# Tile 0 in three pieces through norm, transpose and copy, and whole x tiles on two load queues

## The chip, the cores and the metric

The kernel runs on one core of one Trainium2 chip. The metric is the device time in microseconds (us); lower is better. Engines are named as in the profile: PE is TensorE (PEld its weight loads), DVE is VectorE, ACT is ScalarE, POOL is GpSimd, SP is SyncE, which here only issues transfers (DMAs).

## The reference

A layernorm without affine weights feeds two branches, a linear attention block and a dense block with gelu, and both are added to the input:

```python
def _A_ref(x, wqkv, wo):          # H = 32 heads of 20
    q, k, v = ...                 # x @ wqkv
    phi = lambda t: jnp.where(t > 0, t + 1, jnp.exp(t)) + 1e-6
    pq, pk = phi(q), phi(k)
    kv = jnp.einsum("bhsd,bhse->bhde", pk, v)
    z = jnp.einsum("bhsd->bhd", pk)
    num = jnp.einsum("bhqd,bhde->bhqe", pq, kv)
    den = jnp.einsum("bhqd,bhd->bhq", pq, z)[..., None] + 1e-6
    ...                           # (num / den) @ wo

def _B_ref(x, w1, b1, w2, b2):
    h = _gelu(jnp.einsum("bsd,df->bsf", x, w1) + b1)
    return jnp.einsum("bsf,fd->bsd", h, w2) + b2

xn = _layernorm(x, axis=-1)
return x + _A_ref(xn, A_wqkv, A_wo) + _B_ref(xn, B_w1, B_b1, B_w2, B_b2)
```

x is 2048 tokens by 640 features in bf16; W1 is 640 by 1536 and W2 1536 by 640.

## The kernel before

The 2048 tokens are 16 tiles of 128. A tile of x is loaded with tokens on the 128 partitions, normalised over its 640 features (`xn_tm`), and transposed so that features lie on the partitions (`xnT`, five blocks of 128 features). W1 is held as five rows of blocks, W1 row k being the 128 features that multiply block k of `xnT`, by 1536 outputs. The hidden layer has 12 groups of 128 outputs (`jb`).

All instructions are recorded through a planner, which keeps one list per engine in the order in which the code calls it, and derives the waits from the resources that a step reads and writes. It doesn't reorder: what stands ahead in an engine's list runs first there.

Only the first steps matter for the change. They are:

- Loads. Tile 0 comes in two parts (L272 to L274): columns 0 to 383 by the SP queue and columns 384 to 639 by the ACT queue. Behind its part SP issues tile 1, W1 rows 0, 1 and 2, tile 2, W1 row 3, tile 3, W1 row 4, tiles 4 to 7.
- PE starts with matmuls on constants (`filler`, L319, and L445, which also starts the accumulation in banks 0 to 5), until tile 0 is ready.
- Layernorm of a tile: `ln_half` twice on DVE (a BATCH_NORM_STATS2 on a part of the columns, L351, after the first of which POOL adjusts a number, L354), `ln_aggr` (DVE L359, then on POOL the power -0.5 that gives `rstd`, L361), and `ln_norm` (DVE L373). Tile 0 is normalised in two pieces, of 256 and 384 columns.
- `transp2` (L336) transposes a tile on PE, blocks 0 and 1 into PSUM bank 6 and blocks 2 to 4 into bank 7. `copy2` moves them to `xnT`, the first part on ACT (L344), the second on DVE (L345). Tiles 0 and 1 go this way. Tile 2 is transposed by `transp` (L381) and copied on DVE (L389); from tile 3 on a DMA transposes.
- The head of the hidden layer is written row by row: `hk` (L431) does, for one group jb, the matmuls of the rows `ks` on one or two tiles. Groups 2b and 2b+1 share bank b; when row 4 is done, ACT applies gelu (L438).

The order of PE's work is the list `plan` (L464 to L468): for tile 0 row 0 of W1 over 12 groups; "B1", a small transpose of b1 (L325) with its copy on ACT; row 1; "T1", tile 1's transposes; row 2; for tile 1 rows 0, 1, 2; for both tiles row 3 on groups 0 to 7; "T2", tile 2's transposes; the remaining rows. Then come packs of four groups for tiles 2 and 3 (`h_pack`, L415), and units of 256 or 512 tokens (`h_unit`, L400), up to about 59 us. The attention and the output follow. PSUM banks of these later groups are dealt out in a ring by `take`, which `at(n)` sets.

The order of DVE's work ahead of the plan is the sequence of calls at L450 to L459; more follows at "T1" and "T2" inside the loop over the plan (L490 to L507).

Of the kernel before, what the change touches and what calls it, by code (L numbers as in the profile page):

```python
# [6 lines left out]
ACT = mybir.ActivationFunctionType  # L7
P = 128
FP32 = mybir.dt.float32
BF16 = mybir.dt.bfloat16  # L10
# [102 lines left out]
def bass_parallel_sum__linear_attn_block__dense_activation_gelu__prompt_kernel(  # L113
    nc: bass.Bass, A_x, A_wqkv, A_wo, B_x, B_w1, B_b1, B_w2, B_b2, out):
    Batch, S, D = A_x.shape
    F = B_w1.shape[1]
    assert Batch == 1 and D == 640 and F % P == 0 and S % 512 == 0
    NT = S // P
# [3 lines left out]
    DT = D // P  # L122
# [3 lines left out]
    HW = D // 2  # L126
# [11 lines left out]
    Pl = Planner(nc)  # L138
    R_ = Pl.res

    with contextlib.ExitStack() as es:
# [3 lines left out]
        x_in = xPK  # L145
        PK = xPK
        xn_tm = sb("xn_tm", [P, NT, D], BF16)
        xnTf = sb("xnT", [P, DT * S], BF16)
        xnT = xnTf[:].rearrange("p (k s) -> p k s", k=DT)
# [22 lines left out]
        ident = sb("ident", [P, P], BF16)  # L172
# [5 lines left out]
        stats = sb("stats", [P, 4, 12], FP32)  # L178
# [19 lines left out]
        B_ = [R_("bank%d" % i) for i in range(8)]  # L198
# [10 lines left out]
        def bank(b, lo=0, hi=512):  # L209
            return ps[:, b * 512 + lo: b * 512 + hi]  # L210

        def halves(ap):
            return ap.rearrange("p (a n) -> p a n", a=2)

        r_x = [[R_("x%d_%d" % (t, i)) for i in range(2 if t == 0 else 1)] for t in range(NT)]
        r_xr = [R_("xr%d" % c) for c in range(NC)]
        r_xb = [R_("xb%d" % t) for t in range(NT)]
        r_xn = [[R_("xn%d_%d" % (t, i)) for i in range(2 if t == 0 else 1)] for t in range(NT)]
        r_xnT = [[R_("xnT%d_%d" % (t, i)) for i in range(2 if t < 2 else 1)] for t in range(NT)]
        r_W1 = [R_("W1_%d" % k) for k in range(DT)]  # L220
        r_Wk = R_("Wk")
        r_Wq, r_Wv, r_W2 = R_("Wq"), R_("Wv"), R_("W2")
# [3 lines left out]
        r_ident, r_small, r_ones, r_masks, r_hmask = (  # L226
            R_("ident"), R_("small"), R_("ones"), R_("masks"), R_("hmask"))
        r_stats = [[R_("stats%d_%d" % (i, h)) for h in range(2)] for i in range(4)]
# [20 lines left out]
        xv = A_x.rearrange("b s d -> (b s) d")  # L249
# [5 lines left out]
        v = "vector"  # L255
        s_ = "scalar"
        pe = "tensor"

        def dma(eng, dst, src, writes, reads=()):
            Pl.ins(eng, lambda e: e.dma_start(dst, src), reads=reads, writes=writes, dma=True)  # L260
# [4 lines left out]
        def dma_x(t, n):  # L265
            dma("sync", x_in[:, t:t + n, :], xv[t * P:(t + n) * P, :].rearrange("(t p) d -> p t d", p=P),
                sum(r_x[t:t + n], []))

        def dma_w1(k):
            dma("sync", W1[:, k, :], w1v[:, k, :], [r_W1[k]])  # L270

        XA = 3 * P  # L272
        for i, (lo, hi) in enumerate(((0, XA), (XA, D))):
            dma(("sync", s_)[i], x_in[:, 0, lo:hi], xv[0:P, lo:hi], [r_x[0][i]])  # L274
        dma_x(1, 1)
        dma_w1(0)
        dma_w1(1)
        dma_w1(2)
# [15 lines left out]
               reads=[r_ident], writes=[r_ident])  # L294
# [28 lines left out]
        def b1_step():  # L323
            b = take(1)
            Pl.ins(pe, lambda e: e.transpose(bank(b).bitcast(BF16)[:, 0:JT], b1tmp[:], ident[:JT, :JT]),  # L325
                   reads=[r_b1tmp, r_ident], writes=[B_[b]])
            Pl.ins(s_, lambda e: e.activation(b1c[:], bank(b).bitcast(BF16)[:, 0:JT], ACT.Copy),
                   reads=[B_[b]], writes=[r_b1c])

        KA = 2  # L330
        TC = KA * P

        def transp2(t, b0, b1):
            for lo, hi, b in ((0, KA, b0), (KA, DT, b1)):
                pT = bank(b).bitcast(BF16)
                Pl.ins(pe, [(lambda e, k=k, pT=pT, lo=lo: e.transpose(  # L336
                    pT[:, (k - lo) * P:(k - lo + 1) * P], xn_tm[:, t, k * P:(k + 1) * P], ident[:]))
                    for k in range(lo, hi)], reads=[r_xn[t][0 if lo == 0 else -1], r_ident], writes=[B_[b]])

        def copy2(t, b0, b1):  # L340
            tok = slice(t * P, (t + 1) * P)
            pA = bank(b0).bitcast(BF16)[:, 0:TC].rearrange("p (k q) -> p k q", q=P)
            pB = bank(b1).bitcast(BF16)[:, 0:D - TC].rearrange("p (k q) -> p k q", q=P)
            Pl.ins(s_, lambda e: e.activation(xnT[:, 0:KA, tok], pA, ACT.Copy), reads=[B_[b0]], writes=[r_xnT[t][0]])  # L344
            Pl.ins(v, lambda e: e.tensor_copy(xnT[:, KA:DT, tok], pB), reads=[B_[b1]], writes=[r_xnT[t][1]])  # L345

        def ln_half(t, h):
            s = t % 4
            cut = XA if t == 0 else HW
            lo, hi = ((0, cut), (cut, D))[h]  # L350
            Pl.ins(v, lambda e: e.bn_stats(stats[:, s, 6 * h:6 * h + 6], x_in[:, t, lo:hi]),  # L351
                   reads=[r_x[t][min(h, len(r_x[t]) - 1)]], writes=[r_stats[s][h]])
            if h == 0:
                Pl.ins(g, lambda e: e.tensor_single_scalar(stats[:, s, 2:3], stats[:, s, 2:3], D * EPS, ALU.add),  # L354
                       reads=[r_stats[s][0]], writes=[r_stats[s][0]])

        def ln_aggr(t):
            s = t % 4
            Pl.ins(v, lambda e: e.bn_aggr(aggr[:, s, :], stats[:, s, :]),  # L359
                   reads=r_stats[s], writes=[r_aggr[s]])  # L360
            Pl.ins(g, lambda e: e.tensor_tensor(out=rstd[:, t:t + 1], in0=aggr[:, s, 1:2], in1=mhalf[:], op=ALU.pow),  # L361
                   reads=[r_aggr[s], r_small], writes=[r_rstd[t]])

        def ln_stats(t):
            ln_half(t, 0)
            ln_half(t, 1)
            ln_aggr(t)

        def ln_norm(t):
            s = t % 4  # L370
            for i, r in enumerate(r_xn[t]):
                lo, hi = (0, D) if len(r_xn[t]) == 1 else ((0, TC), (TC, D))[i]
                Pl.ins(v, lambda e, lo=lo, hi=hi: e.tensor_scalar(  # L373
                    xn_tm[:, t, lo:hi], x_in[:, t, lo:hi], aggr[:, s, 0:1], rstd[:, t:t + 1],
                    ALU.subtract, ALU.mult),
                    reads=r_x[t] + [r_aggr[s], r_rstd[t]], writes=[r])
# [19 lines left out]
        def h_unit(t0, n, jb):  # L396
# [12 lines left out]
               writes=[r_b1c])  # L409
# [14 lines left out]
        def at(b):  # L424
            ring[0] = b

        def hk(t, n, jb, ks):
            b = jb // 2
            o = (jb % 2) * 2 * P + t * P
            tok = slice(t * P, (t + n) * P)  # L430
            Pl.ins(pe, [(lambda e, k=k: e.matmul(  # L431
                bank(b, o, o + n * P), W1[:, k, jb * P:(jb + 1) * P], xnT[:, k, tok],
                start=False, stop=(jb % 2 == 1 and k == DT - 1))) for k in ks],
                reads=[r_W1[k] for k in ks] + [r_xnT[u][0 if max(ks) < KA else 1] for u in range(t, t + n)],
                writes=[B_[b]])
            if DT - 1 in ks and jb % 2:
                for i in range(2):
                    Pl.ins(s_, lambda e, i=i, jb=jb - 1 + i: e.activation(  # L438
                        HG[:, jb, tok], bank(b, i * n * P, (i + 1) * n * P), ACT.Gelu_apprx_tanh, bias=b1c[:, jb:jb + 1]),
                        reads=[B_[b], r_b1c], writes=[r_HG[u][jb - 1 + i] for u in range(t, t + n)])  # L440
# [3 lines left out]
        for b in range(6):  # L444
            Pl.ins(pe, lambda e, b=b: e.matmul(  # L445
                bank(b), nc.const_aps.tensor(1.0, [P, P], BF16), pm[:].broadcast_to((P, 512)), start=True, stop=False),
                reads=[r_pm], writes=[B_[b]])
# [3 lines left out]
        ln_half(0, 1)  # L451
        ln_aggr(0)
        ln_half(1, 0)
        ln_norm(0)
        ln_half(1, 1)
        ln_aggr(1)
        transp2(0, 6, 7)
        copy2(0, 6, 7)
        ln_norm(1)  # L459

        h_list = lambda t, n, lo, hi: [(t, n, jb) for jb in range(lo, hi)]
        k_list = lambda t, n, ks, lo=0, hi=JT: [(t, n, jb, ks) for jb in range(lo, hi)]
# [26 lines left out]

        for u in plan:  # L490
            if u == "B1":
                at(6)
                b1_step()
            elif u == "T1":
                transp2(1, 6, 7)
                copy2(1, 6, 7)
                ln_stats(2)
                ln_norm(2)
                ln_stats(3)
            elif u == "T2":  # L500
                at(6)
                b = transp(2)
                xnT_copy(2, b)
                ln_norm(3)
                xnT_dma(3)
                ln_stats(4)
                ln_rest()  # L507
            elif len(u) == 2:
                h_pack(*u)
            elif len(u) == 4:  # L510
                hk(*u)
            else:
                h_unit(*u)
# [29 lines left out]
        for c in range(NC):  # L543
            ts = range(c * CH, c * CH + CH)
            cc = slice(c * CW, (c + 1) * CW)
            for t in ts:
                b = take(1)
# [3 lines left out]
                    reads=r_xnT[t] + [r_Wk], writes=[B_[b]])  # L551
                phi(bank(b), b, 1, PK[:, t, 0:MW], r_PK[t], r_x[t])
            b = take(1)
# [3 lines left out]
                reads=sum((r_xnT[t] for t in ts), []) + [r_Wk], writes=[B_[b]])  # L557
            phi(bank(b), b, 1, PKT[:, cc], r_PKT[c], [])
            dma_t("sync", PK[:, c * CH:(c + 1) * CH, MW:D], PKT[:, cc], [r_PKr[c]] + sum((r_x[t] for t in ts), []),
                  reads=[r_PKT[c]])  # L560
# [12 lines left out]
        for k in range(DT):  # L573
            for i in range(DT):
                Pl.ins(g, lambda e, k=k, i=i: e.tensor_copy(plain(Wqkv[:, k, D:2 * D], i), parts(Wqkv[:, k, 0:D], i)),  # L575
                       reads=[r_Wq], writes=[r_Wk, r_WqP])
# [165 lines left out]
        b0 = take(2)  # L742
# [67 lines left out]
        for c, bs in ((1, (3, 4, 5, 0, 6)), (2, (7, 1, 2, 3, 4))):  # L810
            bs = [bb[i] for i in bs]
            for t in range(c * CH, c * CH + CH):
                b = bs[t % CH]
# [13 lines left out]
        t = NT - 1  # L827
        xb(t)
        tok = slice(t * P, (t + 1) * P)
        for i, (lo, hi, b) in enumerate([(0, 3 * P, bb[1]), (3 * P, MW, bb[2])]):  # L830
            r_o = R_("ol%d" % i)
            out_mm(t, 0, NS, [(lo, hi)], [b])
            s = t % 2
            Pl.ins(v, lambda e, lo=lo, hi=hi, b=b: e.tensor_tensor(
                out=out_sb[:, s, lo:hi], in0=bank(b, 0, hi - lo), in1=x_res[:, t, lo:hi], op=ALU.add),
                reads=[B_[b], r_xb[t]], writes=[r_o] + ([r_out[s]] if i == 0 else []))
# [41 lines left out]
```

## Time and profile before

| what | us |
|---|---|
| median of 3 runs (lowest to highest) | 207.03 (206.75 to 207.31) |
| the profiled execution | 206.52 |
| its span from the first to the last instruction | 204.8 |
| PE busy in the span | 200.1 |
| clock granted to PE | 1.0 throughout |

Each profile line is read as follows. In the chain of work that ended last, a line is a start, a length, and the instruction (engine, tile written, source line, count) that set the end at that time. In the DMA view a line is destination and source, the queue that issued it, the count, the size of one, and the median time from issue to landing. In the table of stretches come, for each stretch, its length, the busy time of PE, PEld, DVE, ACT and POOL with the number of instructions, the granted clock, the mean busy share of the 16 DMA engines, and GB/s. Times are from the start of the span.

### The profile page before, as it was taken

The numbers are of one execution on the slowest core, as the hardware profiler recorded it, in microseconds if no ns is written. First come the engines' busy times: TensorE is split into PE (matmuls) and PEld (weight loads), VectorE is DVE, ScalarE is ACT, GpSimd is POOL, SyncE is SP. The second block draws the span as 40 slices with busy tenths as digits, with TensorE's granted clock in tenths as the row PEclk, the third lists the DMA queues.
The fourth block names the chain that finished last, engine by engine and source line by source line (L and its number), as shares of the span: only waits on it lengthen the run. The fifth ranks groups of instructions, "written<-read, shape, count | busy, mean of one in ns | idle before, by whom it ended". The sixth has DMA issues, their size and how long they took to land.

```text
span 204.8 us, 3356 instructions
## 1 busy us (share of the span) xinstructions
PE 200.1 (98%) x1226; PEld 105.3 (51%) x1243; DVE 108.5 (53%) x238; ACT 70.7 (35%) x139; POOL 33.1 (16%) x85
## 2 busy tenths in 40 slices
PE   8899999999999999999999999999999999999995
PEld 3799866544444444444546444544444444444443
DVE  3687099200007898399858889534623923513131
ACT  2159977666676555121153554500000000000000
POOL 3234056720000000896000200000000000000000
PEclk9999999999999999999999999999999999999999
DMA  6945956889940111100010000228986531102301
GB/s 161 384 126 92 166 169 126 101 289 321 372 168 0 26 26 26 29 0 0 0 32 5 0 0 15 92 48 192 334 201 137 143 53 53 51 26 51 78 29 51
DMA packets 34457, 21.37 MB, mean 104 GB/s; under 512 B 21384, under 2 KB 33800, under 8 KB 34440
## 3 DMA queue, kind: packets, MB, share of 16 engines
q1 hardware_dynamic: 30384, 17.54, 32.9%
q10 hardware_dynamic: 4056, 3.61, 6.5%
q8 instruction: 10, 0.16, 0.3%
q14 instruction: 7, 0.06, 0.1%
HBM read 13.08 MB, written 2.62 MB: 77 GB/s over the span
## 4 chain that ended last, share of the span: by engine, by line
PE 95%; DMA 1%; ACT 1%; DVE 1%; issue 1%; POOL 0%; DVEq 0%
PE ps L755 29%; PE ps L400 20%; PE ps L634 10%; PE ps L548 8%; PE ps L581 8%; PE ps L766 7%; PE ps L431 3%; PE ps L415 2%; PE ps L590 2%; PE ps L554 2%; DMA xPK<-in_A_x_dram 1%; PE ps L644 1%; ACT Msb L670 1%; PE ps L698 1%; DVE stats L351 0%
## 5 line engine op out<-in xcount | busy, mean ns | idle before, releaser
L755 PE MATMUL ps<-W,HG 128*128 128x512 bf16 (+2 forms) x200 | 43.5, 366 | 0.3 <-ACT Msb L670 0.2
L400 PE MATMUL ps<-xnT,W 128*128 128x512 bf16 (+1 forms) x246 | 41.3, 327 | 0.2
L400 PEld LDWEIGHTS ps<-xnT,W 128*128 128x128 bf16 x250 | 24.3, 98 | 16.6
L404 ACT ACTIVATE HG<-ps,b1c 128x512 bf16<-128x512 f32 (+1 forms) x50 | 28.6, 631 | 11.4 <-PE ps L400 10.6
L755 PEld LDWEIGHTS ps<-W,HG 128*128 128x128 bf16 x204 | 19.5, 98 | 22.2 <-ACT Msb L670 0.2
L536 ACT ACTIVATE ek<-ps 128x512 bf16<-128x512 f32 x40 | 23.8, 597 | 19.4 <-PE ps L634 10.5
L537 DVE TENSOR_SCALAR ek<-ek 128x512 bf16<-128x512 bf16 x40 | 11.5, 288 | 27.0 <-ACT ek L536 27.0
L779 DVE TENSOR_TENSOR W<-ps,xnT 128x512 bf16<-128x512 f32 x15 | 10.4, 691 | 25.0 <-PE ps L755 19.3
L634 PE MATMUL ps<-xnT,Wqkv 128*128 128x512 bf16 x98 | 21.6, 379 | 0.1
L755 PE MATMUL ps<-Msb,PQ 128*128 128x512 bf16 (+2 forms) x84 | 19.5, 366 | 0.1
L351 DVE BATCH_NORM_STATS2 stats<-xPK 128x6 f32<-128x320 bf16 (+2 forms) x32 | 14.0, 477 | 8.0 <-DMA xPK<-in_A_x_dram 8.0
L548 PE MATMUL ps<-Wqkv,xnT 128*128 128x512 bf16 x80 | 17.9, 379 | 0.0
L581 PE MATMUL ps<-xPK,xn_tm 128*128 128x512 bf16 x79 | 17.4, 379 | 0.1
L575 POOL COPY Wqkv<-Wqkv 128x128 bf16<-128x128 bf16 x25 | 13.0, 519 | 22.4 <-PE ps L554 20.9
L634 PEld LDWEIGHTS ps<-xnT,Wqkv 128*128 128x128 bf16 x100 | 9.7, 98 | 11.4
L539 DVE SCALAR_TENSOR_TENSOR PQ<-ps,ek 128x512 bf16<-128x512 f32 x20 | 13.8, 692 | 2.1
L755 PEld LDWEIGHTS ps<-Msb,PQ 128*128 128x128 bf16 x85 | 8.2, 98 | 9.2
L548 PEld LDWEIGHTS ps<-Wqkv,xnT 128*128 128x128 bf16 x80 | 7.8, 98 | 9.4
L581 PEld LDWEIGHTS ps<-xPK,xn_tm 128*128 128x128 bf16 x80 | 7.8, 98 | 9.4
L539 DVE SCALAR_TENSOR_TENSOR xPK<-ps,ek 128x512 bf16<-128x512 f32 x16 | 11.1, 692 | 1.7
L604 DVE TENSOR_TENSOR Msb<-Msb,xPK 128x640 f32<-128x640 f32 x14 | 11.6, 825 | 0.5
L361 POOL TENSOR_TENSOR rstd<-aggr,mhalf 128x1 f32<-128x1 f32 x16 | 9.9, 621 | 8.1 <-DVE aggr L359 8.1
(79 smaller groups left out, 149.3 us busy)
## 6 DMA issues: line engine op xcount, KB each, us to landing
Wqkv<-in_A_wqkv_dram SPq DMA_DIRECT2D x3, 800.0 KB, 6.5
xnT<-in_A_x_dram SPq DMA_DIRECT2D x4, 512.0 KB, 6.5
W<-in_B_w_dram SPq DMA_DIRECT2D x5, 384.0 KB, 5.2
W<-in_B_w_dram SPq DMA_DIRECT2D x1, 1920.0 KB, 12.5
out_dram<-W ACTq DMA_DIRECT2D x15, 128.0 KB, 1.8
xn_tm<-rden ACTq DMA_DIRECT2D x12, 128.0 KB, 3.7
xPK<-in_A_x_dram SPq DMA_DIRECT2D x4, 320.0 KB, 5.1
Wo<-in_A_wo_dram SPq DMA_DIRECT2D x8, 160.0 KB, 7.9
```

Source lines behind the costliest of these rows:

```text
L351: Pl.ins(v, lambda e: e.bn_stats(stats[:, s, 6 * h:6 * h + 6], x_in[:, t, lo:hi]), reads=[r_x[t][min(h, len(r_x[t]) - 1)]], writes=[r_stat ...
L400: Pl.ins(pe, [(lambda e, k=k: e.matmul(bank(b, 0, w), W1[:, k, jb * P:(jb + 1) * P], xnT[:, k, tok], start=(k == 0), stop=(k == DT - 1))) ...
L404: Pl.ins(s_, lambda e: e.activation(HG[:, jb, tok], bank(b, 0, w), ACT.Gelu_apprx_tanh, bias=b1c[:, jb:jb + 1]), reads=[B_[b], r_b1c], wri ...
L536: Pl.ins(s_, lambda e: e.activation(e2, src, ACT.Exp), reads=br, writes=[r_ek[s]])
L539: Pl.ins(v, lambda e: e.scalar_tensor_tensor(out=d2, in0=src, scalar=0.0, in1=e2, op0=ALU.max, op1=ALU.add), reads=br + [r_ek[s]], writes= ...
L548: Pl.ins(pe, [(lambda e, k=k, b=b, t=t: e.matmul(bank(b), xnT[:, k, t * P:(t + 1) * P], Wqkv[:, k, D:D + MW], start=(k == 0), stop=(k == D ...
L575: Pl.ins(g, lambda e, k=k, i=i: e.tensor_copy(plain(Wqkv[:, k, D:2 * D], i), parts(Wqkv[:, k, 0:D], i)), reads=[r_Wq], writes=[r_Wk, r_WqP])
L581: Pl.ins(pe, lambda e, t=t, b=b, f=f, i=i: e.matmul(bank(b), xn_tm[:, t, f * P:(f + 1) * P], PK[:, t, 0:MW], start=(i == 0), stop=(i == NT ...
L604: Pl.ins(v, lambda e, t=t: e.tensor_tensor(out=zsum, in0=zsum, in1=PK[:, t, :], op=ALU.add), reads=[r_PK[t], r_PKr[t // CH], r_zsum], writ ...
L634: Pl.ins(pe, [(lambda e, k=k, j=j, b=b: e.matmul(bank(b), Wqkv[:, k, D + j * P:D + (j + 1) * P], xnT[:, k, cc], start=(k == 0), stop=(k == ...
L755: Pl.ins(pe, [(lambda e, i=i, x=x, bk=bk: e.matmul(bank(bk, 0, x[1] - x[0]), seq[i][0], seq[i][1][:, x[0]:x[1]], start=(i == 0), stop=(i = ...
L766: Pl.ins(pe, lambda e, i=i: e.matmul(bank(b), seq[i][0], seq[i][1], start=(i == 0), stop=(i == NS - 1)), reads=seq[i][2], writes=[B_[b]], ...
```

## The change

- Tile 0 is loaded whole by SP, tile 1 whole by ACT, and W1 rows 0 to 2 follow directly behind tile 0 on SP. Both statistics of tile 0 take 320 columns, as for the other tiles.
- Tile 0 is normalised in pieces of 128 and 512 columns, and transposed and copied in three parts: block 0 (bank 6, ACT), blocks 1 and 2 (bank 7, ACT), blocks 3 and 4 (bank 6, DVE). Tile 1 is transposed in parts of three blocks (bank 6, ACT) and two (bank 7, DVE).
- Both statistics of tile 1 stand ahead of tile 0's normalisation on DVE. Part 2 of tile 0 is transposed and copied at "B1", that is between the matmuls of rows 0 and 1, and tile 1's normalisation follows that copy. Tile 3's statistics stand ahead of tile 2's normalisation.
- `hk` waits for the part of `xnT` that holds the block of its row. B1 and T2 take bank 7 instead of 6.

```diff
-        XA = 3 * P
-        for i, (lo, hi) in enumerate(((0, XA), (XA, D))):
-            dma(("sync", s_)[i], x_in[:, 0, lo:hi], xv[0:P, lo:hi], [r_x[0][i]])
-        dma_x(1, 1)
+        for t, eng in enumerate(("sync", s_)):
+            dma(eng, x_in[:, t, :], xv[t * P:(t + 1) * P, :], r_x[t])
         dma_w1(0)
         dma_w1(1)
         dma_w1(2)
...
-        KA = 2
-        TC = KA * P
-
-        def transp2(t, b0, b1):
...
-        def copy2(t, b0, b1):
+        PARTS = [((6, 0, 1, s_), (7, 1, 3, s_), (6, 3, DT, v)), ((6, 0, 3, s_), (7, 3, DT, v))]
+
+        def xT(t, k):
+            return r_xnT[t][next(i for i, (_, lo, hi, _) in enumerate(PARTS[t]) if lo <= k < hi)]
+
+        def tr_part(t, i):
+            b, lo, hi, _ = PARTS[t][i]
+            pT = bank(b).bitcast(BF16)
+            Pl.ins(pe, [(lambda e, k=k: e.transpose(
+                pT[:, k * P:(k + 1) * P], xn_tm[:, t, k * P:(k + 1) * P], ident[:]))
+                for k in range(lo, hi)], reads=[r_xn[t][min(i, len(r_xn[t]) - 1)], r_ident], writes=[B_[b]])
+
+        def cp_part(t, i):
+            b, lo, hi, eng = PARTS[t][i]
             tok = slice(t * P, (t + 1) * P)
...
+            src = bank(b).bitcast(BF16)[:, lo * P:hi * P].rearrange("p (k q) -> p k q", q=P)
+            Pl.ins(eng, lambda e: e.activation(xnT[:, lo:hi, tok], src, ACT.Copy) if eng == s_ else
+                   e.tensor_copy(xnT[:, lo:hi, tok], src), reads=[B_[b]], writes=[r_xnT[t][i]])
...
-                lo, hi = (0, D) if len(r_xn[t]) == 1 else ((0, TC), (TC, D))[i]
+                lo, hi = (0, D) if len(r_xn[t]) == 1 else ((0, P), (P, D))[i]
...
-                reads=[r_W1[k] for k in ks] + [r_xnT[u][0 if max(ks) < KA else 1] for u in range(t, t + n)],
+                reads=[r_W1[k] for k in ks] + [xT(u, k) for u in range(t, t + n) for k in ks],
...
         ln_half(1, 0)
+        ln_half(1, 1)
         ln_norm(0)
-        ln_half(1, 1)
         ln_aggr(1)
-        transp2(0, 6, 7)
-        copy2(0, 6, 7)
-        ln_norm(1)
+        tr_part(0, 0)
+        cp_part(0, 0)
+        tr_part(0, 1)
+        cp_part(0, 1)
...
             if u == "B1":
-                at(6)
+                at(7)
                 b1_step()
+                tr_part(0, 2)
+                cp_part(0, 2)
+                ln_norm(1)
             elif u == "T1":
-                transp2(1, 6, 7)
-                copy2(1, 6, 7)
+                for i in range(2):
+                    tr_part(1, i)
+                    cp_part(1, i)
                 ln_stats(2)
+                ln_half(3, 0)
+                ln_half(3, 1)
                 ln_norm(2)
-                ln_stats(3)
+                ln_aggr(3)
             elif u == "T2":
-                at(6)
+                at(7)
```

More of the change, by code (lines that the diff above doesn't have):

```diff
@@ L213, in halves @@
             return ap.rearrange("p (a n) -> p a n", a=2)
-        r_x = [[R_("x%d_%d" % (t, i)) for i in range(2 if t == 0 else 1)] for t in range(NT)]
+        r_x = [[R_("x%d" % t)] for t in range(NT)]
         r_xr = [R_("xr%d" % c) for c in range(NC)]
@@ L218, in bass_parallel_sum__linear_attn_block__dense_activation_gelu__prompt_kernel @@
         r_xn = [[R_("xn%d_%d" % (t, i)) for i in range(2 if t == 0 else 1)] for t in range(NT)]
-        r_xnT = [[R_("xnT%d_%d" % (t, i)) for i in range(2 if t < 2 else 1)] for t in range(NT)]
+        r_xnT = [[R_("xnT%d_%d" % (t, i)) for i in range((3, 2)[t] if t < 2 else 1)] for t in range(NT)]
         r_W1 = [R_("W1_%d" % k) for k in range(DT)]
@@ L328, in b1_step @@
                    reads=[B_[b]], writes=[r_b1c])
-        KA = 2
-        TC = KA * P
-        def transp2(t, b0, b1):
[L334 to L338, printed above, removed]
@@ L341, in copy2 @@
+        def cp_part(t, i):
+            b, lo, hi, eng = PARTS[t][i]
             tok = slice(t * P, (t + 1) * P)
[L342 to L345, printed above, removed]
+            src = bank(b).bitcast(BF16)[:, lo * P:hi * P].rearrange("p (k q) -> p k q", q=P)
+            Pl.ins(eng, lambda e: e.activation(xnT[:, lo:hi, tok], src, ACT.Copy) if eng == s_ else
+                   e.tensor_copy(xnT[:, lo:hi, tok], src), reads=[B_[b]], writes=[r_xnT[t][i]])
@@ L347, in ln_half @@
         def ln_half(t, h):
             s = t % 4
[L349 to L352, printed above, removed]
+            Pl.ins(v, lambda e: e.bn_stats(stats[:, s, 6 * h:6 * h + 6], x_in[:, t, h * HW:(h + 1) * HW]),
+                   reads=r_x[t], writes=[r_stats[s][h]])
             if h == 0:
```

## The prediction

> **What bounds the kernel now.** I read the page's busy shares first, then the chain that ended last (its totals and its first pieces in order of time), then the timeline of the first 14 us, then the DMA issues one by one, and last the table of half-microsecond stretches.
>
> The busy shares and the totals of the chain:
>
> ```profile
> PE 200.1 (98%) x1226; PEld 105.3 (51%) x1243; DVE 108.5 (53%) x238; ACT 70.7 (35%) x139; POOL 33.1 (16%) x85
> ...
> PE 95%; DMA 1%; ACT 1%; DVE 1%; issue 1%; POOL 0%; DVEq 0%
> ```
>
> TensorE (PE) carries 95% of the chain. The change reorders work that ends in the first 12 us, so two questions matter: when TensorE's unbroken stream begins, and whether a hole opens in it. The chain in order of time (start, length, what):
>
> ```profile
> 0.81 2.30 DMA xPK<-in_A_x_dram
> 3.11 0.02 issue
> 3.13 0.90 DVE stats L351 x2
> ...
> 4.12 0.22 DVE aggr L359
> 4.34 0.07 issue
> 4.42 0.58 POOL rstd L361
> ...
> 5.09 0.36 DVE xn_tm L373
> 5.45 0.05 issue
> 5.50 0.30 PE ps L336 x2
> 5.80 0.02 issue
> 5.82 0.39 ACT xnT L344
> 6.21 0.14 issue
> 6.35 0.83 PE ps L431 x12
> 7.18 0.11 PE ps L325
> 7.29 0.78 PE ps L431 x12
> 8.06 0.28 PE ps L336 x5
> 8.34 3.55 PE ps L431 x56
> ```
>
> Until 6.35 the end is set by a latency chain on tile 0: load, two statistics, aggregate, power on GpSimd, normalise 256 columns, two transposes, one ScalarE copy. From 6.35 TensorE goes on without a gap, and everything later rides on that start. Nothing after about 14 us is touched except which PSUM bank a group takes.
>
> The loads that compete at the start are three of x and the first weight row (operation count, size, us from issue to landing, one issue a line, in order of issue on SP):
>
> ```profile
> xPK<-in_A_x_dram SPq DMA_DIRECT2D x1, 96.0 KB, 2.3
> xPK<-in_A_x_dram SPq DMA_DIRECT2D x1, 160.0 KB, 2.3
> W<-in_B_w_dram SPq DMA_DIRECT2D x1, 384.0 KB, 4.0
> ```
>
> Tile 0's first part is issued at 0.81 and lands at 3.11; its second (64 KB on ACT's queue, 2.5 us) at 3.31; tile 1, issued at 1.24, lands at 3.54; W1's row 0, issued at 1.73, lands at 5.73. Rows 1 and 2 land at about 6.9 and 7.87 in the same view (2.2 + 4.7, 2.67 + 5.2). Their first users start at 7.29 and 8.34, so no weight row is the last wait now. The stretches (PE to POOL busy, clock, DMA share, GB/s):
>
> ```profile
> 2.50:3.00 0.50, 0.50 (x3) 0.22 (x2) 0.00 (x0) 0.24 (x2) 0.00 (x0) 1.00 0.98 312
> 3.00:3.50 0.50, 0.50 (x3) 0.23 (x2) 0.37 (x1) 0.00 (x0) 0.00 (x0) 1.00 1.39 165
> 3.50:4.00 0.50, 0.50 (x3) 0.16 (x2) 0.50 (x2) 0.00 (x0) 0.22 (x1) 1.00 0.74 154
> ```
>
> The transfer engines are full when the x tiles arrive (0.98), and move least just after, from 3.0 to 4.0, when W1's row 0 begins.
>
> [...]the two parts of tile 0, on two queues, land 0.2 us apart although they differ by half in size. [...]So the order in which the code lists DVE's work is the order it runs. The trace shows it: the second statistic of tile 1 (5.65) starts after both pieces of tile 0's normalisation although its data landed at 3.54. [...]here it is 1.00 in every stretch with PE gaps of 0.37 and 0.22 us.
>
> **The change part by part.**
>
> *Loads.* Now 64 KB of tile 0 go by ACT and 96 KB by SP, then tile 1 by SP. Afterwards tile 0's 160 KB go by SP and tile 1's 160 KB by ACT, both issued at about 0.81. All of tile 0 must land before the first statistic starts, where today 96 KB are enough. The 320 KB of both tiles end at 3.54 today on full engines; sharing evenly, they should again end near 3.5[...]. Bounds for tile 0: 3.11 (tile 1 steals nothing) to 3.54 (perfectly even). I take 3.38, so the first statistic starts at 3.40 in place of 3.13: **+0.27** (0 to +0.43). All of SP's later issues, W1's rows, x2 and x3, come one issue (about 0.45 us) earlier; the engines are nearly full from 4.5 on (344 GB/s and more), so rows land 0 to 0.45 us earlier. Their users wait for other things, so this is worth nothing. b1's 3 KB now follow 160 KB on ACT's queue instead of 64; they are needed at 7.18, some 3.5 us later: nothing.
>
> *Statistics.* Two of 320 columns (pitch 0.40, from the pair at 8.65 that takes 0.88) instead of 384 and 256 (0.89 together): nothing.
>
> *Both statistics of tile 1 ahead of tile 0's normalisation.* DVE is free from 4.25 and idle from 4.69 to 5.09 for the power on GpSimd (0.57). One more statistic with pitch 0.40 fits: 4.25 + 0.80 = 5.05. The gap of 0.40 is just used up; nothing, with up to +0.1. What queues behind them on DVE is the normalisation, so tile 1 must have landed when the first one starts, 1.12 us after tile 0's first. That is the slower rival below.
>
> *Part 0 of one block.* Chain from normalisation to the first W1 matmul, before: 0.36 + 0.05 + 0.30 + 0.02 + 0.39 + 0.14 = 1.26. After: the normalisation of 128 columns about 0.32 (256 columns take 0.346, 384 take 0.374: 0.03 per block); one transpose 0.22 instead of two 0.30; the copy of one block about 0.30. For the copy the trace has no such row; the gelus run at a pitch of 4.49/12 = 0.374 for 256 columns and 2.26/8 = 0.283 for 128, thus 0.09 per block (bounds 0 and 0.13). Sum 0.32 + 0.05 + 0.22 + 0.02 + 0.30 + 0.14 = 1.05: **-0.21**. The two transposes of part 1 now stand before the first W1 matmul and need normalisation of the other 512 columns; that ends about 0.64 after the start of the first piece (both pieces take 0.64 now), and with 0.05 and two transposes of 0.056 they are issued at 0.80, inside the 1.05. Hidden by 0.25. The ScalarE copy of part 1 ends about 1.38 after that start, and its reader, row 1's matmuls, comes at 1.05 + 1.05 = 2.1: hidden by 0.7.
>
> *Part 2 inside the stream.* Today all five transposes of tile 0 run before 6.35, the last three while ScalarE copies. Now the last two stand after B1 between the matmuls of rows 0 and 1, on the path: 2 x 0.056 (five take 0.28 at 8.06): **+0.11**.
>
> *Tile 1's normalisation later.* It now queues on DVE behind part 2's copy, which waits for those transposes. Let H be the first W1 matmul. Row 0 takes 0.83, B1 0.11, part 2 0.11, row 1 0.78: PE reaches tile 1's transposes at H + 1.83. Part 2's transposes end at H + 0.94 + 0.06 + 0.22 = 1.22; DVE's copy of 256 columns starts 0.04 later (as at 8.38) and occupies about 0.20 (for 384 the next instruction follows after 0.27): 1.46; normalising 640 columns 0.45: 1.91; 0.05 to PE: 1.96. PE waits **+0.13** (0 to 0.25). Now that normalisation is done at 7.66, 0.40 before PE comes.
>
> *Later reads.* Tile 1's first part is three blocks on ScalarE: transposes, 0.47 for 384 columns and 0.14 end about 0.96 after PE starts T1, and the reader comes after 0.28 + 0.78 = 1.06: hidden by 0.1, the tightest cover here; lost, it costs its excess. Tile 2's normalisation now stands behind both statistics of tile 3: about 2.0 us after T1 begins the power is under way, at 3.0 it is done, and PE comes for tile 2 after 0.28 + 3.55 = 3.83: nothing. The banks of T2 and the packs move by one, so the first pack takes bank 0, last read by the second gelu, which ends at about 13.3; PE arrives at 13.76: nothing. The shift of the ring gives later groups the same distances.
>
> *Sum.* +0.27 - 0.21 + 0.11 + 0.13 = **+0.30 us**. The profiled execution took 206.52 (span 204.8 and 1.7 around it), so it would become 206.8; the three timed runs have the median 207.03, 0.5 above it, and become **207.3**.
>
> **The rivals.** A measurement of this kernel can tell about 0.3%, 0.62 us, from no change: below 206.4 counts as faster, above 207.65 as slower.
>
> 1. *Tile 0 lands as early as now and tile 1's normalisation is in time*: [...]Then 0 - 0.21 + 0.11 + 0 = -0.1: 206.9. For it: the first part of tile 0 started earlier though both issues are at 0.81. Against: a share of 0.98 leaves no room for 64 KB more in front of the statistics.
> 2. *Tile 1 lands late, and DVE waits for it (slower)*. [...]Both statistics of tile 1 stand ahead of tile 0's normalisation on an in-order engine, so from 3.40 + 1.12 = 4.52 on every delay goes on the path in full. With landing at 5.0 it adds 0.5: 207.8. Against it: half of the packets of tile 1 should be through before tile 0 ends, and 1.1 us is a wide cover.
> 3. *The clock falls*. PE is nearly idle from 5.13 to about 6.4. [...]
>
> **How the numbers follow.** The forecast as worked out 0.50, rival 1 0.23, rival 2 0.22, rival 3 0.02, anything else 0.03. The forecast's own spread is the sum of its bounds, about -0.1 to +0.6, with the scatter of a median of runs that spread over 0.56 us. Slower: rival 2 gives 0.17, the forecast's upper tail 0.09, the rest 0.03: 0.29. Faster: the scatter under rival 1 and the unknown: 0.07. Same: 0.64. The range goes from rival 1 less scatter, 206.6, to rival 2 with a little more, 208.0.
>
> **What would show it.** In the profile after: the first statistic starts near 3.40 (3.13 refutes the shared engines); the normalisation starts 1.95 after it (more means tile 1 came late, and the wait before L351 names the load); the first W1 matmul comes 1.05 after that; two transposes stand between rows 0 and 1; a wait of 0.1 to 0.2 stands before tile 1's transposes; then no gap. A stream that starts before 6.2 or after 6.8, or a hole after 12 us, would make the prediction wrong.

## The result, and the profile after

The changed kernel takes 208.41 us (median of 6 runs, 207.43 to 208.80) against 206.94 (6 runs, 206.65 to 207.31) for the kernel before; the ratio is 1.0061 with a 95% interval of 1.0033 to 1.0088. That is slower by 0.3% to 0.9%. The forecast was 207.3, "no change" as the likeliest, with a range of 206.6 to 208.0: the time lies outside it.

The six times are not one heap: two at 207.43 and 207.65, four from 208.35 to 208.80. The profiled execution belongs to the upper four (208.8, span 207.1). Here are its busy shares and the row of the granted TensorE clock, in tenths over 40 slices:

```profile
PE 201.1 (97%) x1226; PEld 106.6 (51%) x1243; DVE 108.1 (52%) x238; ACT 70.9 (34%) x140; POOL 32.6 (16%) x85
...
PEclk9699999999999999999999999999999999999999
```

The same row of the kernel before:

```profile
PEclk9999999999999999999999999999999999999999
```

TensorE's busy time is only 1.0 us above that of before (200.1), although the span grew by 2.3. The new thing is the 6 in the second slice, from 5.2 to 10.4 us. The chain that ended last shows the head (start, length, what):

```profile
0.81 2.93 DMA xPK<-in_A_x_dram
...
4.76 0.21 DVE aggr L357
4.97 0.76 DVE stats L349 x2
5.73 0.09 DVE xn_tm L371
...
6.79 1.30 PE ps L429 x12
8.10 0.12 PE ps L323
8.22 0.33 PE ps L336 x2
8.54 1.28 PE ps L429 x12
9.82 0.53 PE ps L336 x5
10.36 3.63 PE ps L429 x56
```

The first W1 matmul starts at 6.79 against 6.35. Then the 12 matmuls of W1 row 0 take 1.30 us in place of 0.83, those of row 1 1.28 in place of 0.78, and row 2 on tile 0 begins at 10.36 against 8.34. So 0.44 us are lost ahead of the stream and 1.58 us within its first 3.6 us. After that the stretches equal those of before to about 0.3 us in all. The half-microsecond stretches of the same execution say why (length, busy PE to POOL, clock, DMA share, GB/s):

```profile
4.50:5.00 0.50, 0.07 (x2) 0.00 (x0) 0.39 (x3) 0.00 (x0) 0.07 (x1) 1.00 0.87 350
5.00:5.50 0.50, 0.00 (x0) 0.00 (x0) 0.50 (x2) 0.00 (x0) 0.45 (x1) 1.00 1.21 289
5.50:6.00 0.50, 0.00 (x0) 0.00 (x0) 0.48 (x3) 0.00 (x0) 0.32 (x2) 1.00 0.52 209
6.00:6.50 0.50, 0.30 (x3) 0.17 (x3) 0.49 (x3) 0.13 (x1) 0.00 (x0) 1.00 0.96 344
6.50:7.00 0.50, 0.42 (x6) 0.27 (x7) 0.00 (x0) 0.40 (x2) 0.43 (x1) 0.97 1.05 399
7.00:7.50 0.50, 0.50 (x9) 0.50 (x7) 0.00 (x0) 0.13 (x1) 0.14 (x1) 0.50 1.03 333
...
10.00:10.50 0.50, 0.50 (x9) 0.50 (x7) 0.10 (x1) 0.32 (x1) 0.00 (x0) 0.61 1.05 389
```

TensorE has nothing to do from about 4.5 to 6.1, and from 6.97 to 10.38 it gets half its clock (0.50). The record of the kernel before has no such stretch. It begins only at 4.70, however, where the clock first rises, so "throughout" in the table of the kernel before means from there on: before that, its six constant matmuls of 512 columns took 2.76 us (0.46 each), while 20 of that width take 4.32 (0.22 each) later in the same trace. It starts at about half speed too. In the changed kernel's trace the clock rises at 3.56.

### The profile page after: what moved, and what is told of

It reads as the page before. It is cut to its first block, busy times and chain, and to the rows that moved or that the text cites. A ratio compares the mean times of both kernels' runs of the same rounds, so it can differ in the third digit from the quotient of the medians.

```text
span 207.1 us, 3351 instructions
## 1 busy us (share of the span) xinstructions
PE 201.1 (97%) x1226; PEld 106.6 (51%) x1243; DVE 108.1 (52%) x238; ACT 70.9 (34%) x140; POOL 32.6 (16%) x85
## 4 chain that ended last, share of the span: by engine, by line
PE 94%; DMA 1%; DVE 1%; issue 1%; ACT 1%; DVEq 0%
PE ps L760 28%; PE ps L398 20%; PE ps L639 10%; PE ps L553 8%; PE ps L586 8%; PE ps L771 7%; PE ps L429 4%; PE ps L413 2%; PE ps L595 2%; PE ps L559 2%; DMA xPK<-in_A_x_dram 1%; DVE stats L349 1%; PE ps L649 1%; ACT Msb L675 1%; PE ps L703 1%
## 5 line engine op out<-in xcount | busy, mean ns | idle before, releaser
L784 DVE TENSOR_TENSOR W<-ps,xnT 128x512 bf16<-128x512 f32 x15 | 10.4, 691 | 25.0 <-PE ps L760 19.4
L349 DVE BATCH_NORM_STATS2 stats<-xPK 128x6 f32<-128x320 bf16 x32 | 13.9, 476 | 9.2 <-DMA xPK<-in_A_x_dram 9.2
L580 POOL COPY Wqkv<-Wqkv 128x128 bf16<-128x128 bf16 x25 | 12.5, 501 | 22.4 <-PE ps L559 20.9
```

## The experiments

The theories at the start: C, TensorE's idle time ahead of tile 0's transposes costs a stretch at half clock (3.41 us in the first trace) in a part of the executions; L, the later landing of tile 0 is the whole loss; P, the pieces and the new order are. Later came S (tile 0 is late because it shares the engines with tile 1) against W (a whole tile in one transfer is late by itself). From here on "dipped" is an execution above 208.22 us; in each of the five that were traced, half clock lay over the head. The limit was set when the times were known. Of the 29 executions that it picks out below, 11 have a fall of the clock on record (a mean of 0.992 over the span); the other 18 read 1.000, and only one of these was traced. So for most of them half clock is inferred from the time. The kernel with 20 constant matmuls, which is late for another reason, is left out of this count.

**The changed kernel again, five times.** No edit.

> The changed kernel once more, for a second trace and the spread of its runs. Theory C (clock): the times fall in two groups, near 207.5 where TensorE keeps its clock through the head and near 208.6 where it runs a window of 3.4 us at half speed; the trace shows either first W1 matmuls at a pitch of about 0.11 us (slow) or of about 0.066 us (quick). Theory L (loads alone): one group, and tile 0's first statistic always near 3.75, with every later step keeping its distance to it.

22 runs: 18 from 206.90 to 207.66 (median 207.25), 4 from 208.50 to 208.87; median of all 207.33, ratio 1.0019 (1.0002 to 1.0035), beside 54 runs of the kernel before with median 207.17. The trace, of an execution at 208.62, has the clock at 0.992 and the same stretch of 3.41 us at half clock as the first one: row 0 takes 1.24. Theory C's two groups are there, though the other three slow executions read 1.000.

> The changed kernel once more, for a trace of its quicker group. Theory C: if it takes about 207.3, no window at half clock is in it and the head's 12 matmuls of row 0 take 0.83 us; if it takes about 208.6, a window at 0.5 lies over them and they take about 1.25 us.

This one took 207.22 and shows the changed kernel without a dip; its chain:

```profile
3.61 0.90 DVE stats L349 x2
...
5.57 0.09 DVE xn_tm L371
...
6.63 0.83 PE ps L429 x12
7.46 0.11 PE ps L323
7.57 0.23 PE ps L336 x2
7.80 0.02 issue
7.82 0.04 DVE xnT L345
7.86 0.17 issue
8.03 0.45 DVE xn_tm L371
8.48 0.05 issue
8.53 0.45 PE ps L336 x5
8.98 3.55 PE ps L429 x56
```

Row 2 starts at 8.98, which is 1.38 earlier than in the dipped trace. The remaining difference to before, 0.64, is the forecast's mechanism: a later first statistic, and DVE's copy and normalisation standing on the path ahead of tile 1's transposes.

> The changed kernel once more, for a trace. Theory C: either near 207.3 with row 0's matmuls in 0.83 us, or near 208.6 with a slow head: where no fall of the clock is on record (1.000 over the span), the constant matmuls and the first W1 matmuls run at half speed until the record begins.

> The changed kernel, for a trace. Theory C: near 207.3 with row 0's 12 matmuls in 0.83 us, or near 208.6 with 1.2 us or more for them and half speed in or just before them.

207.17 and 207.40, both without a dip, row 0 in 0.83. Their first statistics start at 3.34 and 3.67.

> The changed kernel, for one more trace. Theory C: near 207.3 with row 0's 12 matmuls in 0.83 us, or near 208.6 with 1.2 us or more for them.

208.23 us, above the limit, and a recorded clock of 1.000 over the whole span. TensorE's timeline in it (start, length, what, idle time before):

```profile
2.08 2.76 PE L443 MATMUL ps<-pm,const-bfloat16-1.0 128*128 128x512 bf16 x6
4.64 0.74 PE L317 MATMUL ps<-const-bfloat16-1.0 128*128 128x128 bf16 x5
5.87 0.71 PE L336 MATMUL ps<-ident,xn_tm 128*128 128x128 bf16 x3 [0.49 <-DVE xn_tm L371]
6.61 1.44 PE L429 MATMUL ps<-xnT,W 128*128 128x128 bf16 x12
```

Here the matmuls were never quick before the head: 12 of row 0 take 1.44, or 0.12 each, where a trace without a dip has 0.83 (0.07 each). The record of the clock starts only when it first rises, at 9.91 here, so a head that is slow throughout reads 1.000. Both kinds of dip cost about the same (row 2 on tile 0 begins at 10.36 and at 10.18): in the first the clock rose early (the constant matmuls in the trace at 208.8 ended at 4.56) and fell, in the second it had not yet risen. Why it hadn't is not shown: the gap of 0.49 is shorter here than in two quick traces of the same kernel (0.69 and 0.86). Of the changed kernel's nine dips only two have the fall on record, so most may be of this second kind.

**More constant matmuls ahead of the transposes.** 20 for 5:

```diff
-        filler(5, P)
+        filler(20, P)
```

> The changed kernel with 20 instead of 5 constant matmuls ahead of tile 0's transposes, so that TensorE is idle about 0.6 us less there. Theory C: no stretch at clock 0.5, the head's first W1 matmuls at 0.066 us each, median 207.2 to 207.7, that is 0.8 to 1.3 below the changed kernel. Theory L: nothing is gained, 208.3 to 208.6, since the loads are the same.

A miss for C on the face of it: 208.88 (9 runs, 207.97 to 209.49). The trace has no dip, row 0 takes 0.83, and row 2 starts at 8.98 as in the 207.22 trace. But TensorE stands still later:

```profile
18.98 2.23 PE ps L413 x40
21.21 0.94 issue
22.15 7.80 PE ps L398 x70
```

The unit at 22.15 is the first on tiles 4 and 5. In the DMA view tile 5's transpose, issued at 17.65, took 4.4 us to land here and 2.5 in the 207.22 trace, where TensorE came at the same time, 21.21, and didn't wait. So the edit has a side effect, and this kernel says nothing on the median. The next run keeps the number of instructions:

```diff
-        filler(5, P)
+        filler(5)          # 512 columns wide
```

> The changed kernel with its 5 constant matmuls 512 columns wide instead of 128, so that TensorE is busy about 0.8 us longer before tile 0 while the number of instructions stays. Theory C: the slower group near 208.6 vanishes (none or one of the runs), median 207.1 to 207.4. Theory F (the 0.94 us wait at 21.2 us of the kernel with 20 constant matmuls comes from an instruction load moved by 15 more instructions): no such wait before the units of tiles 4 and 5. Rival of F: TensorE's earlier arrival brings the wait, so it is here too, and the time is 208 or above.

22 runs, 206.92 to 208.21, none dipped, median 207.50, ratio 1.0016 (1.0003 to 1.0029). Two runs, at 208.18 and 208.21, lie just under the limit, but no group stands apart. The trace holds no record of the clock; row 0 takes 0.83. The wait at 21.2 is gone (tile 5's transpose lands in 2.6), with the stream just as early, so it goes with the 15 more instructions (one trace of each). The load of instructions that the DMA view shows at 20.1 to 20.5 in this trace and in the 207.22 one came before 19.7 with 20 matmuls, that is while tile 5's transpose was under way; that fits, but no run moved it alone. The dips vanished, as C says. The median missed C's 207.1 to 207.4. It did not fall, for its ratio to the kernel before is about that of the changed kernel (1.0019), where 4 of 22 were dips, and it lies above the 207.25 of that kernel's quick runs. The trace shows a wait of 0.34 us at 35.85; whether that is the reason was not tried.

**Taking the constant matmuls away.** From the kernel before, and from the changed kernel:

```diff
-        filler(5, P)
```

> The kernel before without its 5 constant matmuls of 128 columns just ahead of tile 0's transposes, so that TensorE is idle about 0.9 us there in place of 0.4. Theory C: a group of slow executions 1.2 to 1.5 us above the others appears, in a tenth to a third of the runs, the rest stays at 206.6 to 207.6. Rival (the half clock belongs to the new pieces and loads, not to the gap): one group as before, median within 0.3 us of it.

4 of 14 runs at 208.27 to 209.14 and one at 208.03, the rest from 206.47 to 207.28. The chain of an execution at 208.55 (clock 0.992):

```profile
1.73 4.97 DMA W<-in_B_w_dram
6.70 0.05 issue
6.75 0.84 PE ps L431 x12
7.59 0.11 PE ps L325
7.70 0.01 issue
7.71 1.43 PE ps L431 x12
9.14 0.53 PE ps L336 x5
```

None of the new pieces or loads is in this kernel, and the dip is there, over row 1. So a dip does not need the new code. TensorE idles twice in this execution: 0.71 us before the transposes and 0.72 for W1's row 0, which landed at 6.70. Two of the four have the fall on record.

> The changed kernel without the 5 constant matmuls ahead of tile 0's transposes: TensorE idle from about 4.6 to 5.9 us. Theory C: 40 to 80 of 100 executions are slow (208.3 and more), the rest at 207.0 to 207.6; a slow trace with a recorded clock of 1.000 shows the constant matmuls and the W1 matmuls of the head at half speed, with the record beginning only where they become quick. Rival: the share stays near a quarter, then the slow executions don't come from the idle time.

> The changed kernel without the 5 constant matmuls once more, for a second trace. Theory C: slow with the head's first W1 matmuls at about twice 0.066 us each, or near 207.3 with none of them so.

All 6 of the first are dipped (208.34 to 208.88; five of them with clock 0.992), ratio 1.0072 (1.0045 to 1.0100); the seventh took 207.22. In the dipped trace TensorE idles 1.62 us, from 4.36; in the other, where the clock rose later and the accumulation matmuls ended at 4.84, 1.29 us.

**The loads.** First the old loads under the new pieces, then the reverse edit on the kernel before, that is the new loads under the old pieces. The split of tile 0's statistics (384 and 256 columns, or twice 320) goes with the loads and is not shown:

```diff
-        for t, eng in enumerate(("sync", s_)):
-            dma(eng, x_in[:, t, :], xv[t * P:(t + 1) * P, :], r_x[t])
+        XA = 3 * P
+        for i, (lo, hi) in enumerate(((0, XA), (XA, D))):
+            dma(("sync", s_)[i], x_in[:, 0, lo:hi], xv[0:P, lo:hi], [r_x[0][i]])
+        dma_x(1, 1)
...
```

> The changed kernel with the loads and the statistics' cut of the kernel before (tile 0 in two parts on two queues, tile 1 behind on SP); the three pieces and the new orders stay. Theories C and L both: tile 0's first statistic back at 3.13, first W1 matmul near 6.15, TensorE idle before its first transpose about 0.4 us, no fall of the clock, 206.8 to 207.2. Rival P (the pieces and the new order cost the time): it stays at 207.8 or above.

207.09 (22 runs), ratio 1.0006 (0.9990 to 1.0022), 4 dipped. In its trace the first W1 matmul starts at 6.11, where W1's row 0 had landed at 6.06, and row 2 at 8.47. By its median rival P falls: the pieces and the order cost nothing in a quick execution. But C and L expected no fall of the clock here, and 4 of 22 dipped (one with the fall on record), against 2 of 149 of the kernel before under the same loads. So the pieces and the order seem to bring dips of their own; how is not shown, for the one trace is of a quick execution.

> The kernel before with only the new loads (tile 0 whole on SP, tile 1 whole on ACT, statistics of 320 columns). Theory L: first statistic 0.3 to 0.6 later, 207.3 to 207.6. Theory C: the same delay makes TensorE idle for 0.7 to 1.0 us before the first transpose, so some executions lose a window at half clock: median 207.5 to 208.6, in two groups. Rival P: no more than 207.1.

207.18 (14 runs), ratio 1.0001 (0.9983 to 1.0018), 2 dipped (208.44 and 208.77), TensorE idle for 0.99 before the transposes in its trace, first statistic at 3.54. The median lies below what C (207.5 to 208.6) and L (207.3 to 207.6) expected. So the new loads alone don't make it slower either, and 2 of 14 are dips.

**Tile 1 back on SP, behind tile 0.**

```diff
-        for t, eng in enumerate(("sync", s_)):
+        for t, eng in enumerate(("sync", "sync")):
```

> The changed kernel with tile 1 on SP behind tile 0 instead of on ACT's queue. Theory S[...]: the first statistic starts at 3.1 to 3.2, the first W1 matmul at 6.1 to 6.2 or when row 0 of W1 has landed. Rival W (a whole tile in one transfer starts or ends late by itself): still 3.5 to 3.6. Theory C adds that the idle time ahead of the transposes shrinks to 0.4 to 0.5 us, and the slower group to a tenth of the runs or less; median 206.9 to 207.3 under S.

206.95 (22 runs, 2 dipped), ratio 1.0006 (0.9989 to 1.0024). Its chain begins:

```profile
0.81 2.25 DMA xPK<-in_A_x_dram
3.06 0.02 issue
3.08 0.90 DVE stats L349 x2
```

Tile 0, whole and in one transfer, lands at 3.06. Rival W falls: one transfer of the whole tile is not late by itself. Theory S fits: in the changed kernel's first trace, from 2.5 to 3.0 us, SP's queue takes 48.3% of the 16 engines' time and ACT's 44.3%. But the edit does a second thing: W1's row 0, next on SP, is issued at 1.73 again instead of 1.27. So the delay of 0.5 us came from tile 1 on the other queue, from row 0 close behind, or from both. The two runs counted as dips, 208.90 and 209.03, lie 2 us above the median, more than the 1.35 us of a dip in the changed kernel; they read 1.000 and were not traced.

**Tile 1's normalisation ahead of part 2's copy.**

```diff
-                cp_part(0, 2)
                 ln_norm(1)
+                cp_part(0, 2)
```

> The changed kernel with tile 1's normalisation ahead of the copy of part 2 on DVE (the two lines swapped), so that it no longer waits for part 2's transposes. It measures the size of that wait. Theory: TensorE's unit of row 2 on tile 0 starts 2.1 to 2.15 us after the first W1 matmul in place of 2.35 (row 0 0.83, b1 0.11, part 2 0.11 to 0.23, row 1 0.78, tile 1's transposes 0.28); with a span of 205.0 to 205.6 if the clock stays full. Rival: 2.3 or more, then the loss lies in the transposes on the path themselves.

One run, 207.34. Row 2 starts 2.10 after the first W1 matmul (8.79 and 6.69), as expected, against 2.35 in the 207.22 trace (and in the other two quick ones): the wait for tile 1's normalisation is worth 0.25 us.

**Both of these edits, and the constant matmuls 256 wide.**

```diff
-        filler(5, P)
+        filler(5, 2 * P)
```

> Both edits together (tile 1 on SP behind tile 0, its normalisation ahead of part 2's copy), and the 5 constant matmuls 256 wide, to see whether the pieces gain once their losses are taken away. Theory: row 2 on tile 0 starts near 8.25 against 8.34 to 8.54 in the kernel before, so 0.1 to 0.3 less; part of it is lost at the wait near 36 us for tiles 10 and 11: median 206.8 to 207.1, a tie with the kernel before within its scatter. Rival: W1's rows land later than their users and hold it at 207.2.

206.63 (22 runs, 206.29 to 207.74, none dipped) against 206.89 of the kernel before (43 runs): ratio 0.9979 (0.9966 to 0.9993). It is faster than the kernel before by 0.1% to 0.3%, and by more than was expected (206.8 to 207.1); the changed kernel's 32 executions have the median 207.45. How much each of the three edits gives was not taken apart. Its chain from the first statistic:

```profile
3.12 0.90 DVE stats L349 x2
...
6.15 0.83 PE ps L429 x12
...
8.25 3.55 PE ps L429 x56
```

**The kernel before once more.**

> The kernel before, unchanged, for a second trace of it, because its timed runs here (median 207.17) lie 0.65 above its profiled execution (206.52). Theory D (tile 0's landing varies from execution to execution, whatever the loads): the first statistic comes later than 3.13 and the first W1 matmul later than 6.35, the span being longer by the same amount. Rival: the head is the same within 0.1 us, and the difference lies later.

207.56. The rival is nearly right for the first matmul (6.31, statistics as in the first trace), but the chain shows two waits after it:

```profile
2.19 5.18 DMA W<-in_B_w_dram
7.37 0.05 issue
7.42 0.84 PE ps L431 x12
...
33.92 1.64 PE ps L400 x15
35.56 0.69 issue
36.25 1.80 PE ps L400 x15
```

W1's row 1 landed at 7.37 and held TensorE for 0.17, so row 2 begins at 8.54, not 8.34; and at 35.56 the unit on tiles 10 and 11 waits 0.69 for its input. The second wait is absent in the first trace of before and is 0.03 in the 207.22 trace of the changed kernel, whose TensorE arrives at 35.88. A head later by up to 0.69 would have cost this execution nothing (an estimate from this wait).

The dips over all runs, with TensorE's idle time ahead of tile 0's first transpose in the few traces of each kernel. This time depends on the clock as well: where the clock rose at 3.56, the constants ended at 4.56, and where it rose at 4.70, at 5.13.

| kernel | idle, us | dipped | fall on record |
|---|---|---|---|
| before | 0.35 and 0.37 | 2 of 149 | 1 |
| changed, constants 512 wide | 0.46 | 0 of 22 | 0 |
| combined | 0.56 | 0 of 22 | 0 |
| changed, tile 1 on SP | 0.60 | 2 of 22 | 0 |
| before, no constants | 0.71 | 4 of 14 | 2 |
| before, new loads | 0.99 | 2 of 14 | 0 |
| changed | 0.30 to 1.54 | 9 of 32 | 2 |
| changed, no constants | 1.29 and 1.62 | 6 of 7 | 5 |

The changed kernel with the old loads has 4 of 22 (1 on record); its one trace shows no gap, for the clock rose late in it and the constants lasted until 5.38. The 9 of 32 of the changed kernel are 4 of the first 6 and 5 of the next 26; all 32 have the median 207.45, those without a dip 207.27, the dipped ones 208.62.

What sorts the traces is not the gap alone but how busy TensorE is after the clock rises. Every stretch at half clock on record in the head is 3.41 us long (6.97 to 10.38 in the first trace), and it begins 3.41 us after the first rise. In 15 traces the first rise is on record within the first 6 us. It comes at 3.48 to 5.76, although the first matmul starts at 0.84 in all of them. In the 3.41 us after it TensorE was busy for 1.62 to 1.96 us in the four traces whose clock then fell, and for 2.19 to 3.17 us in the eleven whose clock held. The dip that was never quick before 9.91 is not among them: from 3.08 to 6.50 TensorE was busy for 2.90 of 3.41 us in it, and the clock rose only 3.41 us after that.

## Why the prediction was wrong

*The step that failed* is the third rival: "The clock falls", which was given a chance of 0.02. So low a chance rested on no trace: that of the kernel before shows a clock of 1.00 across gaps of 0.37 and 0.22 us, and no gap as long as the one foreseen. The traces of the changed kernel have it: in the 3.41 us before the clock fell (3.56 to 6.97 in the first trace) TensorE was busy for 1.70 us, half of it, and lost its clock. And the same kernel dips in one execution and not in the next: its clock first rose at 3.48 and 3.56 in the two traces where it fell again, and at 4.73 to 5.76 in the three quick ones; what sets the time of the rise is not shown. That makes a mixture, and by the times a chance of about a quarter (9 of 32), not 0.02. The gap itself was also taken too short. The prediction let it begin at 5.13, where the constants end in the trace before; with the rise at 3.56 they ended at 4.56, and TensorE had nothing to do for 1.54 us. This holds for falls on record, two of the nine dips. In the one other dip that was traced the clock had not risen before the head; why, and whether the gap has a part in it, stays open.

The price is 1.35 us (208.62 against 207.27). A stretch of 3.41 us at half speed holds work that takes 1.7 us at full speed (an estimate from its length), so no more than 1.7 can be lost. By their times four of the first six runs were dips, and with them the median went to 208.41; at the share of the later 22 it was 207.33. So the size of the miss was in part bad luck: at 5 dips in 26, the share of all later runs, four or more in six would come about once in 70 times (an estimate that takes the runs as independent).

*A size that was too small* made the gap longer. The load step, +0.27 with bounds of 0 and +0.43, is right in direction (with tile 1 on SP, and W1's row 0 later with it, the first statistic is back at 3.08) and wrong in size: it starts at 3.34 to 3.80 in the traces of the changed loads, mostly 3.53 to 3.67, that is +0.4 to +0.5. The upper bound stood on the old landing of both tiles, 3.54, and left out that W1's row 0 now follows directly: it is issued at 1.27 and lands at 4.87, and the tiles are under way until 3.74 and 3.9. How the delay divides between tile 1 and row 0 was not tried.

*Statistics and part 0* were right: from the first statistic to the normalisation 1.96 (forecast 1.95), from there to the first W1 matmul 1.06 (forecast 1.05) in the 207.22 trace.

*Part 2 in the stream and tile 1's normalisation*: forecast +0.11 and +0.13, measured +0.36 together (2.35 against 1.99 from the first W1 matmul to row 2), of which 0.11 is left when the normalisation goes first. So the wait was 0.25, the upper bound given: part 2's transposes stand alone and take 0.23 to their end, and tile 1's five take 0.45 after a standstill, not 0.28.

*What was counted as worth nothing*: the earlier W1 rows. In the kernel before they are not always in time (0.17 in its second trace, 0.72 without the constants), so issuing them earlier is worth something in a part of the executions. "Nothing after about 14 us is touched" missed the wait at 35.6, which gives back up to 0.69. Together these may be why +0.64 in the head at full clock shows as +0.1 in the times (207.25 for the 18 runs without a dip, beside 207.17).

*The second rival*, tile 1 landing late, did not come: it landed at 3.9 (0.81 + 3.1), and its statistics start at 4.88 without a wait.

With the clock held, the forecast of 207.3 meets the median of 23 of 32 executions, 207.27. That is partly luck: the head lost 0.64 and not 0.30, and a wait that the prediction did not know gave some of it back. The failure is of a risk that was seen and given 0.02 without a trace of such a gap.

## What to carry to other kernels

Before the first real matmuls, count TensorE's busy time, not only the latency chain: here the clock fell where TensorE was busy for 1.96 us or less of the 3.41 us after the first rise, and held from 2.19 up. Long gaps go with this: kernels whose traces show gaps of 0.35 to 0.6 us dipped in 4 of 215 executions and the one with 1.3 to 1.6 in 6 of 7, but the new pieces under the old loads dipped in 4 of 22 with no gap in their one trace. Let warm-up matmuls (the constants here) end just before the data come, and last longer when the data come later: at 512 columns they left a gap of 0.46 us and none of 22 executions dipped. Widening them removed the dips without the later wait that came with more of them, but did not lower the median by itself. In these traces tile 0 landed at 3.32 to 3.77 with tile 1 on a second queue and the weights close behind, and at 3.06 and 3.09 with tile 1 behind it on the same queue and the weights later: it is worth trying to give the transfer that is needed first the engines to itself. And where times fall into two groups, six runs can misstate their shares; look at a trace of each group before pricing the mean.

## What the runs showed that was not expected

- TensorE busy for half of the 3.41 us after the first rise (1.62 to 1.96 us in four traces) did not keep the clock; the stretch lost lasts 3.41 us (6.97 to 10.38).
- The record of the clock begins with its first rise: an execution with a slow head from the start reads 1.000 (208.23). The traces with 20 constants and with 512 columns have no record at all.
- 15 more instructions on TensorE, which cost no time themselves, went with a wait of 0.94 us 13 us later in the one trace of that kernel, behind a tile's transpose that took 4.4 instead of 2.5 us to land.
- One 384 KB row of W1, issued at 1.73 in each of three executions with the old loads, landed at 5.73, 6.06 and 6.70.
